# Sliding-window attention with ALiBi and an ELU MLP on one core: from two stages to one hand-ordered interleaving

## The chip, the core and the metric

The kernel runs on one of the eight cores of a Trainium2 chip. The core has five engines with an instruction queue each: TensorE (PE, matmuls; its weight loads are shown as PEld), VectorE (DVE), ScalarE (ACT), GpSimd (POOL) and SyncE (SP, which here only issues DMAs). They work on SBUF, the on-chip memory of 128 partitions, and on PSUM, eight banks of 128 x 512 f32 into which PE writes. The engines run side by side and wait for each other through semaphores; each runs its own instructions in their order. The metric is the time of one execution in microseconds of the device.

## What is computed

Attention over 8 batches, 8 heads, 576 positions, head size 64, in a causal window of 128 with a linear bias (ALiBi), then for all 4608 tokens an MLP 512 to 2048 to 512 with ELU (called MoE in the code, though it has one expert). Cut to what matters:

```python
scores = scale * np.matmul(q, k.transpose(0, 1, 3, 2))          # scale = 1 / sqrt(64) = 0.125
rel = pos[:, None] - pos[None, :]
slopes = 2.0 ** (-8.0 * (np.arange(H) + 1) / H)
bias = slopes[:, None, None] * (-np.abs(rel))[None, :, :]
mask = (rel >= 0) & (rel < 128)
attn = softmax(np.where(mask, scores + bias[None], -1e9))       # over keys
x = (attn @ v).transpose(0, 2, 1, 3).reshape(4608, 512)
h = x @ w_in
out = np.where(h > 0.0, h, np.exp(np.minimum(h, 0.0)) - 1.0) @ w_out
```

Inputs and output are f32 in device memory; the matmuls take f16.

## The kernel before

Scores are kept transposed, keys on partitions and queries along the free dimension. The 576 positions are four key blocks of 128 and one of 64. A key block sees queries of its own block and the next, so a head's scores are 128 rows of 256+256+256+192+64 = 1024 columns (`CUM` and `WID` are their starts and widths).

There are two stages, and the second begins when the first has ended. The Tile framework's scheduler sets the order of each engine's queue from the order in which the operations are written and the buffers of the pools; it also makes all semaphores.

Setup: POOL and DVE make an identity matrix and for each head a table `Mh` of bias and mask (L67), 128 x 256. POOL issues the loads of the weights, cast to f16 on the way (L76 for `w_in`, L81 for `w_out`).

Attention, for each batch: POOL issues the loads of q, k and v, cast to f16 (L130, L134, L141, L146). v goes into two tiles, each with 64 columns of ones beside the 64 of v (L140), so that the same matmul that makes the weighted values makes the softmax's denominators. For each pair of heads PE transposes q and k (L158) and ACT copies them to SBUF (L163 to L166). For each head: five score matmuls into PSUM `sp` (L174); DVE scales them and adds bias and mask, three operations `u` (L182, L186, L190); ACT takes Exp into `E` (L194, L195). One head later `do_av` follows: six matmuls of `E` with v and ones into `avp` (L108). For even heads DVE takes the reciprocal of the denominators (L114). For odd heads ACT takes Ln and then Exp of its negative (L117, L118), each with a load of another activation table ahead of it. DVE multiplies and writes the normalized values into `xT` (L119), which holds x transposed, 512 features by 4608 tokens, in f16.

MoE, for each of nine blocks of 512 tokens: for each of 16 chunks of 128 hidden features four matmuls make `hpsum` (L221, four PSUM buffers), ACT takes Relu (`rh`, L229) and Exp (`e`, L231), and DVE makes ELU from both as min(e - 1, rh) (`g`, L233): for h > 0 the smaller is h, for others it is e^h - 1, as the Relu is 0. Two chunks behind, four matmuls (L214) add the chunk into the four accumulators `opsum`, one for each 128 tokens. At a block's end ACT copies these to SBUF (`ob`, L241) and SP issues the stores.

## Time and profile before

| | |
|---|---|
| median of 3 runs | 573.47 us (573.37 to 573.53) |
| span of the profiled execution | 571.8 us, first to last instruction, so some 1.7 us lie around it |
| busy: PE, DVE, ACT, POOL | 448.8, 360.2, 405.4, 192.1 us |
| first matmul | at 26.0 us |
| first MoE matmul | at 308.8 us |
| last attention matmul | ends at about 311 us |
| moved by DMA | 46.14 MB read from device memory, 9.44 MB written |

How to read the profile: a group's row names line, engine, operation, output and inputs, their shapes and the count; behind it stand the time that the group was busy, the mean duration of one in ns, and how long its engine stood idle ahead of such instructions, with what ended that idle time. A line of the windows has the stretch and its length, then busy time and count for PE, PEld, DVE, ACT and POOL, then PE's granted clock, the busy share of the DMA engines and GB/s. A line of the timeline has start, duration from the first to the end of the last, engine, line, operation and count of a run of like instructions. Matmuls overlap: one starts while the one before it still drains, so their durations add up to more than the time that they take.

### The profile page before, as it was taken

Reading aid. Unit: us, or ns where it says so; the run is one execution under the profiler, and the core shown is the slowest. Engines: PE = TensorE matmul, PEld = TensorE weight load, DVE = VectorE, ACT = ScalarE, POOL = GpSimd, SP = SyncE. Lnnn points to the kernel's source line nnn. Section 1 sums busy time; section 2 is a strip of 40 time slices with the busy share of each in tenths; the row PEclk is TensorE's granted clock in tenths of the full one; section 3 lists DMA queues with packets and bytes.
Section 4 is the critical chain, followed back from the end, with each engine's and each line's share of the span. In section 5 each row is a group of like instructions: output and inputs, shape, how many; then the busy total and the mean of one; then the engine's idle time right before and its main releaser. Section 6 shows DMA issues by size and latency. Waiting matters only on the chain.

```text
span 571.8 us, 6352 instructions
## 1 busy us (share of the span) xinstructions
PE 448.8 (78%) x2176; PEld 211.4 (37%) x2176; DVE 360.2 (63%) x442; ACT 405.4 (71%) x709; POOL 192.1 (34%) x285
## 2 busy tenths in 40 slices
PE   0065667767767767767767999999999999999995
PEld 0033333333333333333433444444444444444442
DVE  2047899999999999999998534343434343433342
ACT  0036888888888888888888666666666767676764
POOL 5899996838659384780000000000000000000000
PEclk9999999999999999999999999999999999999999
DMA  7999999959999496990000001101010101010101
GB/s 150 188 109 116 94 106 69 93 33 101 66 71 82 29 107 44 84 83 0 0 1 1 1 37 39 52 23 64 11 74 1 73 1 74 1 73 1 75 1 74
DMA packets 158112, 32.92 MB, mean 58 GB/s; under 512 B 150912, under 2 KB 152960, under 8 KB 158080
## 3 DMA queue, kind: packets, MB, share of 16 engines
q0 software_dynamic: 152896, 23.08, 56.0%
q1 hardware_dynamic: 5184, 9.44, 4.4%
q8 instruction: 17, 0.28, 0.2%
q14 instruction: 15, 0.12, 0.1%
HBM read 46.14 MB, written 9.44 MB: 97 GB/s over the span
## 4 chain that ended last, share of the span: by engine, by line
PE 52%; DVE 29%; ACT 6%; issue 6%; POOL 3%; DMA 3%; ACTq 0%; POOLq 0%
PE opsum L214 21%; DVE rden L114 19%; PE hpsum L221 17%; PE avp L108 7%; PE tp L158 7%; DVE xT L119 4%; DVE u L182 2%; ACT ob L241 2%; DVE u L186 2%; DMA wi<-in_moe_w_in_dram 2%; DVE g L233 1%; ACT e L231 1%; PE sp L174 1%; POOL wo L81 1%; DMA ks<-in_k_dram 1%
## 5 line engine op out<-in xcount | busy, mean ns | idle before, releaser
L233 DVE SCALAR_TENSOR_TENSOR g<-e,rh 128x512 f16<-128x512 f32 x144 | 99.5, 692 | 149.1 <-ACT e L231 149.1
L214 PE MATMUL opsum<-wo,g 128*128 128x512 f16 x576 | 146.2, 379 | 2.4 <-DVE g L233 2.4
L221 PE MATMUL hpsum<-xT,wi 128*128 128x512 f16 x576 | 148.0, 383 | 0.0
L229 ACT ACTIVATE rh<-hpsum 128x512 f16<-128x512 f32 x144 | 87.5, 608 | 70.6 <-PE hpsum L221 69.6
L114 DVE RECIPROCAL rden<-avp 64x576 f32<-64x576 f32 x32 | 120.3, 3761 | 12.6 <-PE avp L108 11.3
L158 PE MATMUL tp<-ident,qs 128*128 128x128 f16 (+1 forms) x160 | 25.4, 291 | 89.8 <-DVE u L190 62.0
L108 PE MATMUL avp<-E,vts 128*128 128x256 f16 (+3 forms) x384 | 80.5, 335 | 14.3 <-ACT E L194 13.1
L231 ACT ACTIVATE e<-hpsum 128x512 f32<-128x512 f32 x144 | 87.2, 605 | 0.0
L214 PEld LDWEIGHTS <-g 128*128 128x128 f16 x576 | 54.9, 98 | 74.6 <-DVE g L233 11.5
L221 PEld LDWEIGHTS <-wi 128*128 128x128 f16 x576 | 56.7, 99 | 68.8 <-issue 1.9
L182 DVE SCALAR_TENSOR_TENSOR u<-sp,Mh 128x768 f32<-128x768 f32 x64 | 61.3, 957 | 31.1 <-PE sp L174 29.7
L194 ACT ACTIVATE E<-u 128x960 f16<-128x960 f32 x64 | 64.2, 1003 | 22.6 <-DVE u L186 22.5
L174 PE MATMUL sp<-qT,kT 64*128 64x256 f16 (+2 forms) x320 | 73.1, 368 | 8.0 <-ACT kT L165 5.2
L141 POOL DMA_DIRECT2D vts<-in_v_dram x64 | 57.7, 902 | 0.0
L108 PEld LDWEIGHTS <-vts 128*128 128x128 f16 (+1 forms) x384 | 36.4, 118 | 56.0 <-issue 42.6
L119 DVE TENSOR_TENSOR xT<-avp,rden 64x576 f16<-64x576 f32 x64 | 48.3, 754 | 8.8 <-ACT rden L118 5.6
L174 PEld LDWEIGHTS <-kT 64*128 64x128 f16 (+1 forms) x320 | 36.0, 126 | 42.9 <-issue 17.5
L158 PEld LDWEIGHTS <-qs 128*128 128x128 f16 (+1 forms) x160 | 14.5, 124 | 100.4 <-DVE u L190 47.0
L163 ACT COPY qT<-tp 128x512 f16<-128x512 f16 x32 | 18.4, 574 | 38.1 <-PE tp L158 38.1
L130 POOL DMA_DIRECT2D qs<-in_q_dram x32 | 28.1, 896 | 44.9 <-PE tp L158 44.7
L117 ACT ACT_TABLE_LOAD x32 | 41.1, 1283 | 0.6
L118 ACT ACT_TABLE_LOAD x31 | 39.8, 1283 | 0.6
(34 smaller groups left out, 311.8 us busy)
## 6 DMA issues: line engine op xcount, KB each, us to landing
out_dram<-ob SPq DMA_DIRECT2D x36, 256.0 KB, 2.4
vts<-in_v_dram POOLq DMA_DIRECT2D x64, 128.0 KB, 3.7
qs<-in_q_dram POOLq DMA_DIRECT2D x32, 128.0 KB, 4.3
ks<-in_k_dram POOLq DMA_DIRECT2D x32, 128.0 KB, 4.2
wi<-in_moe_w_in_dram POOLq DMA_DIRECT2D x4, 512.0 KB, 7.7
wo<-in_moe_w_out_dram POOLq DMA_DIRECT2D x16, 128.0 KB, 4.9
vts<-in_v_dram POOLq DMA_DIRECT2D x16, 64.0 KB, 3.1
qs<-in_q_dram POOLq DMA_DIRECT2D x8, 64.0 KB, 3.9
```

The lines of the kernel that those rows point to most:

```text
L108: nc.tensor.matmul(avp[:, a0:a1], vts[hh][0:nk, kb, hloc, :], em, start=st_, stop=sp_,)
L114: nc.vector.reciprocal(out=rden[o64:o64 + 64, :], in_=avp[o64:o64 + 64, 0:576])
L119: nc.vector.tensor_tensor(out=xT[hp_][p64:p64 + 64, b_ * S:(b_ + 1) * S], in0=avp[p64:p64 + 64, 0:576], in1=rden[o64:o64 + 64, :], op=ALU. ...
L158: nc.tensor.transpose(tp[:, which * NKB + kb, 0:nkk], src[0:nkk, kb, 2 * hp:2 * hp + 2, :], ident[0:nkk, 0:nkk],)
L174: nc.tensor.matmul(sp[0:nk, CUM[kb]:CUM[kb] + WID[kb]], kT2[p64:p64 + D, kb * 128: kb * 128 + nk], qT2[p64:p64 + D, kb * 128: kb * 128 + W ...
L182: nc.vector.scalar_tensor_tensor(out=u[:, 0:768], in0=sp[:, 0:768], scalar=0.125, in1=_bcast_mid(Mh[h % H], 3), op0=ALU.mult, op1=ALU.add,)
L194: nc.scalar.activation(E[:, 0:960], u[:, 0:960], AF.Exp)
L214: nc.tensor.matmul(opsum[ts], glist[fc][:, ts * 128:(ts + 1) * 128], w_out_sb[fc], start=(fc == 0), stop=(fc == 15),)
L221: nc.tensor.matmul(hp_, w_in_sb[kc][:, fc * 128:(fc + 1) * 128], xT[kc][:, tb * TB:(tb + 1) * TB], start=(kc == 0), stop=(kc == 3),)
L229: nc.scalar.activation(rh, hp_, AF.Relu)
L231: nc.scalar.activation(e, hp_, AF.Exp)
L233: nc.vector.scalar_tensor_tensor(out=g, in0=e, scalar=1.0, in1=rh, op0=ALU.subtract, op1=ALU.min)
```

## The change

The two stages become one row of 181 slots. All engines' queues are in the order written in the loop over slots (`manual_schedule`); Tile still makes the semaphores and buffers.

A pair of heads is a unit, and a unit begins every four slots (`APS`), so a batch takes 16 (`ABS`). Block t's hidden chunk fc stands in slot 21 + 16t + fc (`LAG` = 21), and its output matmuls 16 slots later, four in each slot. So slots 0 to 20 have attention alone, 21 to 36 attention and hidden chunks, 37 to 130 attention, hidden chunks and outputs, 131 to 164 hidden chunks and outputs, 165 to 180 outputs. Within a slot the order is: hidden chunk, ELU of the chunk before, attention's tasks, loads, output.

What else differs in the work:

- The bias enters through the contraction. `QK` holds each head's q and k in rows 0 to 63 and in rows 64 to 127 constant rows, made once: key position times slope against 1, 1 times slope against minus query position, and rows of indicators against -30000 that push keys ahead of their query far down. All score matmuls contract over 128 rows. ACT takes Exp straight from PSUM, scaled by 0.125. The exact window is cut afterwards by DVE: a minimum of `E` with `band`, which is 60000 inside the window and 0 outside (`cut`).
- q and k are loaded four positions to a run of 1 KB (f32), so blocks hold positions in a permuted order that the last operations of attention undo. `transposes` copies by DVE, where ACT did it before.
- v is loaded once, in f32, by SP, and cast by POOL into `VP`, which has the ones between an even and an odd head's values.
- Scores of a head are two PSUM tiles of one bank; `ps_s` has two banks in turn for scores and transposes. The last 64 queries of all heads of a batch are collected in one bank (`values_tail`).
- All denominators go through Ln and Exp on ACT, and one activation table that has both is loaded once. No reciprocal and no Relu is left.
- ELU: ACT takes Exp of the hidden chunk, POOL clamps it to [0, 1], DVE takes max(e - 1, h) with h from PSUM. `hp` has two PSUM buffers.
- An output accumulator is one bank: 16 matmuls over four slots for 128 tokens, a copy by ACT, a store by SP.

The diff, cut to its core (the old attention and MoE loops are removed whole):

```diff
-    with tc.tile_pool(name="astage", bufs=2) as astage, \
...
-    TB = 512
...
+    NP = H // 2
+    NFC = FF // 128
+    NTB = NTOK // 512
+    APS = 4
+    ABS = NP * APS
+    LAG = ABS + 5
+    MID = S // 2
...
+    work = ctx.enter_context(tc.tile_pool(name="work", bufs=3))
+    gpool = ctx.enter_context(tc.tile_pool(name="gpool", bufs=2))
+    ps_s = ctx.enter_context(tc.tile_pool(name="ps_s", bufs=2, space=PSUM))
+    ps_v = ctx.enter_context(tc.tile_pool(name="ps_v", bufs=2, space=PSUM))
+    ps_t = ctx.enter_context(tc.tile_pool(name="ps_t", bufs=1, space=PSUM))
+    ps_h = ctx.enter_context(tc.tile_pool(name="ps_h", bufs=2, space=PSUM))
+    ps_o = ctx.enter_context(tc.tile_pool(name="ps_o", bufs=1, space=PSUM))
...
+    QK = const.tile([128, H, 2, 768], F16, name="QK")
+    VP = [const.tile([128, 5, NP, 256], F16, name=f"VP{g}", tag=f"VP{g}") for g in range(2)]
+    w_in_sb = [const.tile([128, FF], F16, name=f"wi{c}", tag=f"wi{c}") for c in range(4)]
+    w_out_sb = const.tile([128, NFC, DM], F16, name="wo")
+    xT = const.tile([128, 4, NTOK], F16, name="xT")
...
+    def cast_v(b, n):
+        p = 128 if n < 4 else 64
+        nc.gpsimd.tensor_scalar(
+            out=VP[b % 2][0:p, n, :, :].rearrange("p a (g c) -> p (a g) c", g=2)[:, :, 0:64],
+            in0=vf.pop((b, n))[0:p, :, :], scalar1=1.0, scalar2=0.0, op0=ALU.mult, op1=ALU.add)
+    nc.scalar.preload_act_table_set("natural_log_exp_and_others")
+    with tc.manual_schedule():
+        for hp in range(NP):
+            for f in load_qk(0, (2 * hp, 2 * hp + 2)):
+                f()
+        for f in load_tail(0):
+            f()
+        make_identity(nc, ident)
...
+        nc.vector.memset(band, BIG)
+        def keep(cols, pattern, base, cm):
+            for h in range(4):
+                r = slice(32 * h, 32 * h + 32)
+                o = band[r, cols]
+                if len(pattern) > 1:
+                    o = o.rearrange("p (n j i) -> p n j i", j=4, i=32)
+                nc.gpsimd.affine_select(out=o, in_=o, compare_op=ALU.is_ge, fill=0.0,
+                                        base=base(h), pattern=pattern, channel_multiplier=cm)
...
+        for t, pr, one in ((TQ, 96, 64), (TK, 64, 96)):
+            nc.vector.memset(t[one:one + 1, :], 1.0)
+            nc.vector.tensor_scalar(
+                out=t[pr:pr + 1, :], in0=posi[pr:pr + 1, :],
+                scalar1=(-1.0 if pr == 96 else 1.0), scalar2=None, op0=ALU.mult)
+        nc.vector.memset(QK[:, :, 1, 512:768], 0.0)
+        for h in range(H):
+            c = 8.0 * 2.0 ** (-8.0 * (h + 1) / H)
+            for w, t, sc in ((1, TK, c), (0, TQ, 1.0)):
+                for d0, s0, n in ((0, 0, 576), (640, 512, 64)):
+                    if h % 2:
+                        nc.vector.tensor_scalar(
+                            out=QK[64:128, h, w, d0:d0 + n], in0=t[64:128, s0:s0 + n],
+                            scalar1=sc, scalar2=None, op0=ALU.mult)
+                    else:
+                        nc.scalar.mul(QK[64:128, h, w, d0:d0 + n], t[64:128, s0:s0 + n], sc)
+        for g in range(2):
+            nc.vector.memset(VP[g][:, 4, :, :], 0.0)
+            nc.vector.memset(VP[g][:, :, :, 64:128], 1.0)
+        for n in range(3):
+            load_v(0, n)
+        for n in range(5):
+            cast_v(0, n)
+            if n < 2:
+                load_v(0, n + 3)
...
+        def transposes(b, hp):
+            t = ps_s.tile([128, 2, 2, 4, 2, 32], F16, name="tp", tag="sps")
+            for g in range(2):
+                for w in (1, 0):
+                    for j in range(2):
+                        nc.tensor.transpose(
+                            t[:, g, w, :, j, :],
+                            stq[b][:, w, 2 * hp + g, 2 * j:2 * j + 2, :].rearrange("p a d -> p (a d)"),
+                            ident)
+            for odd in range(2):
+                r = slice(64 * odd, 64 * odd + 64)
+                nc.vector.tensor_copy(
+                    QK[0:64, 2 * hp:2 * hp + 2, :, 0:512].rearrange(
+                        "p h w (n a i) -> p (h w) n a i", a=2, i=32)[:, :, :, odd, :],
+                    t[r, :, :, :, :, :].rearrange("p h w n a i -> p (h w) (n a) i"))
...
+        def scores(b, hp, g, half):
+            s = ps_s.tile([128, 512], F32, name="sp", tag="sps")
+            kq = QK[:, 2 * hp + g, :, :]
+            c0 = 512 + 128 * (b % 2)
+            if half == 0:
+                mm = [(0, 0, 0, 256), (128, 256, 128, 256)]
+            else:
+                mm = [(256, 0, 256, 256), (384, 256, 384, 128), (384, 384, c0, 64), (c0, 448, c0, 64)]
+            for kc, o, qc, n in mm:
+                nc.tensor.matmul(s[:, o:o + n], kq[:, 1, kc:kc + 128], kq[:, 0, qc:qc + n],
+                                 start=True, stop=True)
+            if half == 0:
+                ex[b, hp, g] = work.tile([128, 1024], F16, name="E", tag="E")
+            nc.scalar.activation(ex[b, hp, g][:, 512 * half:512 * half + 512], s, AF.Exp, scale=0.125)
+        def cut(b, hp, g):
+            e = ex[b, hp, g]
+            nc.vector.tensor_tensor(out=e, in0=e, in1=band, op=ALU.min)
+        def values(b, hp, g):
+            e = ex[b, hp, g]
+            vp = VP[b % 2]
+            a = avt[b, hp, g] = ps_v.tile([128, 512], F32, name="av", tag="av")
+            lo = 64 * g
+            for n, o0, e0, w, st, sp in ((0, 0, 0, 256, True, False), (2, 256, 512, 256, False, False),
+                                         (1, 128, 256, 256, False, False), (3, 384, 768, 128, False, True)):
+                nc.tensor.matmul(a[:, o0:o0 + w], vp[:, n, hp, lo:lo + 128], e[:, e0:e0 + w],
+                                 start=st, stop=sp)
...
+        def log_den(b, hp, g):
+            if g == 0:
+                lden[b, hp] = work.tile([128, 512], F32, name="lden", tag="lden")
+            r = slice(64, 128) if g == 0 else slice(0, 64)
+            nc.scalar.activation(lden[b, hp][r, :], avt[b, hp, g][r, :], AF.Ln)
+        def inv_den(b, hp):
+            rden[b, hp] = work.tile([128, 512], F32, name="rden", tag="rden", bufs=2)
+            nc.scalar.activation(rden[b, hp], lden.pop((b, hp)), AF.Exp, scale=-1.0)
+        def normalize(b, hp, g):
+            r, o = (slice(0, 64), slice(64, 128)) if g == 0 else (slice(64, 128), slice(0, 64))
+            nc.vector.tensor_tensor(
+                out=xT[r, hp, b * S:b * S + 512].rearrange("p (n i j) -> p n j i", j=4, i=32),
+                in0=avt.pop((b, hp, g))[r, :].rearrange("p (n j i) -> p n j i", j=4, i=32),
+                in1=rden[b, hp][o, :].rearrange("p (n j i) -> p n j i", j=4, i=32), op=ALU.mult)
...
+        def hidden(t, fc):
+            p = hps[t, fc] = ps_h.tile([128, 512], F32, name="hp", tag="hp")
+            for c in range(4):
+                nc.tensor.matmul(p, w_in_sb[c][:, fc * 128:(fc + 1) * 128],
+                                 xT[:, c, t * 512:(t + 1) * 512], start=(c == 0), stop=(c == 3))
+            e = es[t, fc] = work.tile([128, 512], F32, name="e", tag="e")
+            nc.scalar.activation(e, p, AF.Exp)
+            nc.gpsimd.tensor_scalar(out=e, in0=e, scalar1=1.0, scalar2=0.0, op0=ALU.min, op1=ALU.max)
+        def elu(t, fc):
+            if t not in gs:
+                gs[t] = gpool.tile([128, NFC, 512], F16, name="g")
+            nc.vector.scalar_tensor_tensor(
+                out=gs[t][:, fc, :], in0=es.pop((t, fc)), scalar=1.0, in1=hps.pop((t, fc)),
+                op0=ALU.subtract, op1=ALU.max)
...
+        def output(t, i):
+            ts, f0 = i // 4, 4 * (i % 4)
+            if f0 == 0:
+                ops[t] = ps_o.tile([128, DM], F32, name="op", tag="op")
+            for fc in range(f0, f0 + 4):
+                nc.tensor.matmul(ops[t], gs[t][:, fc, ts * 128:(ts + 1) * 128], w_out_sb[:, fc, :],
+                                 start=(fc == 0), stop=(fc == NFC - 1))
+            if f0 == 12:
+                ob = work.tile([128, DM], F32, name="ob", tag="ob")
+                nc.scalar.copy(ob, ops[t])
+                r0 = t * 512 + ts * 128
+                nc.sync.dma_start(out[r0:r0 + 128, :], ob)
...
+        units = [(b, hp) for b in range(B) for hp in range(NP)]
+        for u, (b, hp) in enumerate(units):
+            s = APS * u
...
+            at(s, scores, b, hp, 0, 0)
+            at(s, scores, b, hp, 0, 1)
+            at(s + 1, cut, b, hp, 0)
+            if u + 1 < len(units):
+                at(s + 1, transposes, *units[u + 1])
+            if hp == 2 and b + 1 < B:
+                at(s + 3, transposes_tail, b + 1)
+            at(s + 2, scores, b, hp, 1, 0)
+            at(s + 3, values, b, hp, 0)
+            at(s + 3, log_den, b, hp, 0)
+            at(s + 3, scores, b, hp, 1, 1)
+            at(s + 4, cut, b, hp, 1)
+            at(s + 5, values, b, hp, 1)
+            at(s + 5, log_den, b, hp, 1)
+            at(s + 5, inv_den, b, hp)
+            at(s + 5, values_tail, b, hp)
+            at(s + 6, normalize, b, hp, 0)
+            at(s + 6, normalize, b, hp, 1)
+            if hp == NP - 1:
+                at(s + 6, normalize_tail_den, b)
+                at(s + 6, normalize_tail, b)
...
+        for b in range(1, B):
+            for n in range(5):
+                at(ABS * (b - 1) + 2 + 2 * n, load_v, b, n)
+                at(ABS * (b - 1) + 6 + 2 * n, cast_v, b, n)
...
+        transposes_tail(0)
+        transposes(0, 0)
+        nslots = LAG + NTB * NFC + NFC
+        for s in range(nslots):
+            m = s - LAG
+            if 0 <= m < NTB * NFC:
+                hidden(m // NFC, m % NFC)
+            if 0 <= m - 1 < NTB * NFC:
+                elu((m - 1) // NFC, (m - 1) % NFC)
+            for f in tasks.get(s, []):
+                f()
+            for l in loads.get(s, []):
+                do_load(*l)
+            if 0 <= m - NFC < NTB * NFC:
+                output((m - NFC) // NFC, (m - NFC) % NFC)
```

Two places show how the queues change. The first is VectorE. In the program before, at the end of attention, one head's bias (`u`), the reciprocal, the last two normalizations and all the ELU operations `g` behind them stand so:

```order
L182 SCALAR_TENSOR_TENSOR u<-sp,Mh_92 128x768
L186 SCALAR_TENSOR_TENSOR u<-sp,Mh_92 128x192
L190 SCALAR_TENSOR_TENSOR u<-sp,Mh_92 64x64
L114 RECIPROCAL rden<-avp 64x576
L119 TENSOR_TENSOR xT_137<-avp,rden 64x576 x2
L233 SCALAR_TENSOR_TENSOR g<-e,rh 128x512 x144
```

In the changed program VectorE has in the middle of the row, over one unit (`E` are the exponentials that are cut, `g` the ELU results, `tp` and `tpt` the transposes):

```order
L325 SCALAR_TENSOR_TENSOR g_2095<-e_2179,hp_2174 128x512
L288 TENSOR_TENSOR xT_92<-av_2123,rden_2189 64x4x4x32
L288 TENSOR_TENSOR xT_92<-av_2183,rden_2189 64x4x4x32
L325 SCALAR_TENSOR_TENSOR g_2095<-e_2217,hp_2212 128x512
L231 COPY QK_84<-tpt_2244 64x4x2x64 x2
L325 SCALAR_TENSOR_TENSOR g_2095<-e_2240,hp_2235 128x512
L253 TENSOR_TENSOR E_2226<-E_2226,band_83 128x1024
L325 SCALAR_TENSOR_TENSOR g_2095<-e_2280,hp_2275 128x512
L253 TENSOR_TENSOR E_2288<-E_2288,band_83 128x1024
L215 COPY QK_84<-tp_2327 64x4x8x32 x2
```

The ELU operations have moved from behind all of attention to one in each slot, between the cuts, copies and normalizations of a unit.

The second place is POOL near the start. Before, the loads of the weights stand there, with the two mask operations:

```order
masks.py:199 AFFINE_SELECT ident<-ident 128x128
L56 AFFINE_SELECT vmask<-vmask 128x256
L76 DMA wi_94<-in_moe_w_in_dram 128x2048
L60 AFFINE_SELECT vmask<-vmask 128x256
L76 DMA wi_96<-in_moe_w_in_dram 128x2048
```

In the changed program POOL has first issued the loads of batch 0's q and k, and made `band` (36 operations) and the constant rows `TK` and `TQ`; the end of that, the casts of batch 0's v, and the weights stand so:

```order
L173 AFFINE_SELECT TQ_152<-TQ_152 32x2x128
L173 AFFINE_SELECT TQ_152<-TQ_152 32x64
L105 TENSOR_SCALAR VP0_85<-vf_224 128x8x64
L105 TENSOR_SCALAR VP0_85<-vf_229 128x8x64
L105 TENSOR_SCALAR VP0_85<-vf_234 128x8x64
L105 TENSOR_SCALAR VP0_85<-vf_240 128x8x64
L105 TENSOR_SCALAR VP0_85<-vf_246 64x8x64
L381 DMA wi0_87<-in_moe_w_in_dram 128x2048
L381 DMA wi1_88<-in_moe_w_in_dram 128x2048
```

The weights' loads have moved behind q, k, the constant rows and the casts.

338 lines of the change are left out of this document (145 added, 193 removed).

## The prediction

> **What bounds the kernel now.** I read the page first (busy time per engine, the chain that ended last), then the windows by stage, then the groups by shape inside each stage, and last the timeline at a few places. The page:
>
> ```profile
> PE 448.8 (78%) x2176; PEld 211.4 (37%) x2176; DVE 360.2 (63%) x442; ACT 405.4 (71%) x709; POOL 192.1 (34%) x285
> PE 52%; DVE 29%; ACT 6%; issue 6%; POOL 3%; DMA 3%; ACTq 0%; POOLq 0%
> ```
>
> No engine is full over the whole span. The shares are averages over two stages with different limits, as the windows show (busy us of PE, PEld, DVE, ACT, POOL in each stretch):
>
> ```profile
> 0.00:34.00 34.00, 2.77 (x10) 1.03 (x10) 3.40 (x10) 2.23 (x4) 25.65 (x47) 1.00 1.36 166
> 34.00:302.00 268.00, 188.08 (x993) 96.63 (x994) 245.42 (x277) 221.57 (x371) 166.47 (x239) 1.00 1.03 66
> 302.00:314.00 12.00, 8.54 (x33) 3.47 (x32) 10.35 (x10) 9.75 (x13) 0.00 (x0) 1.00 0.00 1
> 314.00:320.00 6.00, 5.38 (x26) 2.32 (x25) 4.79 (x7) 4.95 (x10) 0.00 (x0) 1.00 0.00 0
> 320.00:563.00 243.00, 241.44 (x1109) 107.10 (x1108) 95.54 (x138) 163.87 (x309) 0.00 (x0) 1.00 0.10 35
> 563.00:572.00 9.00, 2.62 (x12) 0.81 (x10) 0.69 (x1) 3.03 (x6) 0.00 (x0) 0.88 0.31 117
> ```
>
> There are 34 us of loading, 280 us of attention (to 314) and 258 us of MoE. In attention DVE is busy 245.42 of 268 us and PE waits for it; in MoE PE is busy 241.44 of 243 and DVE is idle 60% of the time. The groups by shape, attention (40 to 300) first and MoE (316 to 562) second; columns are busy us, mean ns, idle before:
>
> ```profile
> L114 DVE RECIPROCAL rden<-avp 64x576 f32<-64x576 f32 x30 | 112.8, 3761 | 12.0 <-PE avp L108 10.8
> L108 PE MATMUL avp<-E,vts 128*128 128x256 f16 x180 | 60.0, 401 | 10.9 <-ACT E L194 9.7 <-DMA vts<-in_v_dram 1.2
> L182 DVE SCALAR_TENSOR_TENSOR u<-sp,Mh 128x768 f32<-128x768 f32 x60 | 57.5, 958 | 1.4
> L119 DVE TENSOR_TENSOR xT<-avp,rden 64x576 f16<-64x576 f32 x60 | 45.3, 754 | 6.8 <-ACT rden L118 3.6
> L117 ACT ACT_TABLE_LOAD x30 | 38.5, 1283 | 0.5
> L186 DVE SCALAR_TENSOR_TENSOR u<-sp,Mh 128x192 f32<-128x192 f32 x60 | 21.1, 352 | 0.4
> L117 ACT ACTIVATE lden<-avp 64x576 f32<-64x576 f32 x30 | 19.3, 643 | 16.4 <-PE avp L108 16.3
> L108 PE MATMUL avp<-E,vts 128*128 128x64 f16 x59 | 15.4, 261 | 0.0
> L221 PE MATMUL hpsum<-xT,wi 128*128 128x512 f16 x555 | 141.3, 379 | 0.0
> L233 DVE SCALAR_TENSOR_TENSOR g<-e,rh 128x512 f16<-128x512 f32 x142 | 98.1, 692 | 147.1 <-ACT e L231 147.0
> L231 ACT ACTIVATE e<-hpsum 128x512 f32<-128x512 f32 x141 | 85.4, 606 | 0.0
> L221 PEld LDWEIGHTS <-wi 128*128 128x128 f16 x554 | 54.2, 98 | 65.3
> L241 ACT COPY ob<-opsum 128x512 f32<-128x512 f32 x32 | 16.4, 600 | 9.7 <-PE opsum L214 9.7
> ```
>
> The reciprocal alone is 3.76 us per second head. The other thing to see is PE: 256 columns take 401 ns in attention, 512 columns 379 ns in MoE. The timeline gives the distance between starts (whole run less the last matmul, over the rest):
>
> ```profile
> 204.96 0.63 PE L108 MATMUL avp<-E,vts 128*128 128x256 f16 x2
> 204.96 1.29 PE L108 MATMUL avp<-E,vts 128*128 128x256 f16 x6
> 206.06 0.57 PE L158 MATMUL tp<-ident,ks 128*128 128x128 f16 x3
> 310.78 1.47 PE L221 MATMUL hpsum<-xT,wi 128*128 128x512 f16 x3
> 345.93 1.03 PE L221 MATMUL hpsum<-xT,wi 128*128 128x512 f16 x4
> 346.79 1.03 PE L214 MATMUL opsum<-wo,g 128*128 128x512 f16 x4
> 347.66 1.03 PE L221 MATMUL hpsum<-xT,wi 128*128 128x512 f16 x4
> L221 PE MATMUL hpsum<-xT,wi x576: 379/379/634, 308.8 to 562.5; 128*128 128x512 f16 x192
> ```
>
> At 345.93: (1.03-0.38)/3 = 0.217 us for 512 columns, 0.424 ns a column. At 204.96: 0.63-0.42 = 0.21 us for 256; at 310.78, with the longest duration 0.634 of the last row: (1.47-0.63)/2 = 0.42 for 512; both 0.83 ns a column. So PE runs all of attention at half the speed of MoE, though the clock column of the windows says 1.00 in both; and it speeds up at about 314, some 3 us after matmuls begin to run without a break at 310.78. A 64-column matmul is limited otherwise: the last of the six begins at 204.96+1.29-0.26 = 205.99 and the next starts at 206.06, 0.07 us.
>
> **The change part by part.** What goes: 32 reciprocals (120 us), 192 bias operations on DVE (64 x (0.958+0.352) = 84, and a short one each), the table loads (38.5 for half of them), 144 Relu passes on ACT. What comes on DVE: a minimum over 128x1024 per head and two copies of 64x1024 per pair out of PSUM. On POOL: 144 clamps of 128x512 and the casts of v. PE keeps its 1152 MoE matmuls and gets 34 per pair of heads (12 of 256 columns, 12 of 128, 10 of 64: 5248 columns). The program is a row of 181 slots; I cost it in six stretches.
>
> *D, slots 37 to 130 (94 slots), all work interleaved.* Four slots hold one pair (a unit). PE: eight 512-column matmuls a slot take 347.66-345.93 = 1.73 us; the unit's 34 cost 12 x 0.109 + 22 x 0.07 = 2.85, so (4 x 1.73 + 2.85)/4 = 2.44 a slot. The floor is all of them at 0.424 ns a column, 2.22 a unit; the ceiling adds a bare weight load to each, 34 x 0.098 = 3.3 on 2.2, 3.1 a slot with one short wait. DVE: a line through L182 and L186 is 0.15 us + 1.05 ns an element, so 1.23 us for 1024. Four g (2.77), two normalizations (1.38, as g), two minima and two copies (4.92), a quarter of the tails (0.55): 9.6, or 2.40 a slot. Minima and copies have f16 operands, which no DVE row shows; if they ran at double rate they would be 0.69 each and DVE 1.85. I take values between, since the nearest rows are all f32. ACT: eight passes of 0.606, two Ln of 0.6, one Exp and one copy of 0.6: 7.2, or 1.8. POOL, from the rows below: clamps 4 x 0.71, casts 0.9, DMA issues 0.8: 4.5, or 1.1. PE is the longest by little. It restarts after waits for cut scores, for copies and for g; before, such a restart is 0.18 (row at 564.76 below). One per slot: 2.62, **D = 246**, bounds 229 and 291. The hp buffers don't set it: only two, but hidden 1.03, e 0.61, clamp 0.71, g 0.69 and hand-overs of 0.4 are 3.44 us against two slots of 5.2; the slot with two copies ahead of the next g uses up most of that slack.
>
> The start and the end need these rows:
>
> ```profile
> 0.86 0.27 DVE L55 MEMSET vmask<- 128x256 f32 x1 [0.86 <-PEq L257]
> 0.97 0.34 POOL L51 IOTA deltai<- 128x256 int32 x1
> 1.27 0.29 POOL masks.py:199 TENSOR_SCALAR_AFFINE_SELECT ident<-ident 128x128 f16<-128x128 f16 x1
> 1.51 0.45 POOL L56 TENSOR_SCALAR_AFFINE_SELECT vmask<-vmask 128x256 f32<-128x256 f32 x1
> 4.54 2.15 POOL L81 DMA_DIRECT2D wo<-in_moe_w_out_dram  x4
> 20.82 3.52 POOL L130 DMA_DIRECT2D qs<-in_q_dram  x4 [0.17 <-issue]
> 24.31 0.73 POOL L134 DMA_DIRECT2D qs<-in_q_dram  x1
> 564.76 1.04 PE L214 MATMUL opsum<-wo,g 128*128 128x512 f16 x4 [0.18 <-DVE g L233]
> 565.19 2.05 ACT L241 COPY ob<-opsum 128x512 f32<-128x512 f32 x4 [1.21 <-PE opsum L214]
> out_dram<-ob SPq DMA_DIRECT2D x36, 256.0 KB, 2.4
> ```
>
> The two select rows (and their starts: 0.40 from the second to what follows) make POOL about 0.15 us + 1.1 ns an element, 0.71 for 512; a memory fill would be cheaper, and up to double is possible for a clamp of two steps.
>
> *A, to the first score.* q and k now come ahead of the weights, so loading no longer bounds. POOL's row does: ten issues (8 x 0.54 + 2 x 0.73 = 5.8), identity 0.5, 28 selects of 256 or 128 (24 x 0.45 + 4 x 0.29 = 12), eight of 64 (1.8), two iotas (0.8), 15 operations on TK and TQ (10 x 0.45 + 5 x 0.22 = 5.6): with the first 0.7, 27 us. DVE waits for the last, then in its order fills QK (16 pieces; 4 to 8 us), sets VP (2 to 4), its small steps (2 to 4), and copies the first transposes (2.5 to 3.8): 10 to 19, so **A = 42**, 37 to 46. The weights queue behind the casts on POOL; the last of these waits for VP on DVE, so they start near 40 and have until slot 21 (76 us) to land: with batch 1's q and k 5.4 MB in f16, and before, the first 34 us moved 166 GB/s x 34 = 5.6 MB.
>
> *B, slots 0 to 20, attention alone.* PE is at half speed (0.83 ns). Between one minimum and the next of its kind: values 0.75, tails 0.3, transposes 8 x 0.107, two copies 1.4 to 2.5, scores 0.43, Exp 0.61, minimum 0.69 to 1.23, hand-overs 0.6: 5.6 to 7.2 a unit. 5.25 units x 6.4: **B = 34**, 29 to 38. *C, slots 21 to 36, no output matmuls yet:* DVE 1.85 to 2.40 a slot, or PE at half speed (16 x 0.42 + 4.4)/4 = 2.8; I take 2.4: **C = 38**, 30 to 45. *E, slots 131 to 164, MoE alone:* PE 1.73, the two hp buffers 3.44/2 = 1.72, I take 1.78: **E = 60.5**, 59 to 72. The bufs were four before; this cover is gone, and each 0.1 us more in the clamp costs 34 x 0.05 = 1.7. *F, the last 16 slots:* 16 x 0.865 + three turns of the single op bank (drain 0.2, copy 0.6, 0.1) 2.7 + last copy 0.6 + landing 2.4 + close 2.2 (571.8 less 565.19+2.05+2.4): **F = 22**.
>
> Sum: 42+34+38+246+60.5+22 = 442.5 of span. The span before is 571.8 and the median of runs 573.47, 1.7 around it: 444.
>
> A rule against the change stands in the Trainium skill, "GPSIMD Engine Reference", sections 1 and 8: POOL shares its SBUF interfaces with DVE and they contend when a DVE instruction has two SBUF inputs, which the minimum has and g no longer has. No trace here shows both at once. By it, as an estimate, a clamp could be late by a whole minimum; the sum would stay where the slack above covers it.
>
> **The rivals.** (1) POOL's clamp is slow, 1.5 us or more, by its own rate or by the minima holding it up. For: no row has a two-step operation of POOL. Against: the selects. E becomes (2.73+1.5)/2 = 2.1 a slot, +11; in D the late g holds DVE's row and through it a few tenths a slot, 0.2 x 94 = 19: 475. Chance 0.12. (2) The slots don't overlap: each PE wait for DVE or ACT stands in the slot, which is then 1.73 + 6.4/4 = 3.33; D = 313 and the time 511. For: PE's order is fixed, one late operand stops all behind it. Against: every consumer stands at least a slot behind its producer. Chance 0.07. (3) The copies and minima at double rate, short matmuls by columns alone: A 37, B 30, C 30, D 94 x 2.35 = 221, E 59, F 22, 401. Chance 0.06. (4) Slower: PE stays at half speed because short waits break its runs, as in attention before. Then D = 94 x (8 x 0.42 + 1.1) = 419, E = 34 x 3.36 = 114, F 35, C 45, A and B 76: 691. It decides from the point where (573-444)/(691-444) = 0.52 of the work runs so. For: attention before, busy for 188 of 268 us and still half. Against: at half speed D needs 4.46 a slot of PE, far above any other engine, so PE would run unbroken, and that is what raised it at 314. Chance 0.04. The Trainium skill, "TensorE: Matmul & The Clock Gate", Part 1, says that the array's clock is halved by default, released after about 3.4 us of sustained work, and halved again after an idle window; the trace agrees on the release (some 3 us), and shows no second halving in the MoE stage. By this rule rival 4 can only strike stretches with long idle times, A and B, where it stands in the sum already, and C, which would be 45 instead of 38.
>
> **How the numbers follow.** The forecast has 0.70; its terms span 411 to 517 if all fall together, 425 to 470 by independent misses. Range 415 to 492: it takes in rival 1 and leaves out 2, 3 and 4, 0.17. A measurement of this kernel tells about 0.2% from no change. Faster 0.95 (forecast, 1, 2, 3), same 0.01 (rival 4 for about half the time), slower 0.04.
>
> **What would show it.** PE busy nearly all of D with 512-column matmuls of 379 ns, DVE about 85%; first score near 42, first hidden near 76, last attention near 360, output-only from 421. A mean near 630 ns for hidden means rival 4; g waiting for POOL in D means rival 1; PE waiting for DVE in each slot, rival 2. It is wrong if D's slot is outside 2.4 to 3.0 us.

## The result and the profile after

The changed kernel took 432.6 us (median of 4 runs, 431.75 to 432.81) against 573.44 for the kernel before beside it: a ratio of 0.754, with a 95% interval of 0.753 to 0.7552. The forecast was 444. The profiled execution took 432.81 with a span of 431.1, so 1.7 us lie around it, as before.

From the page of the kernel after, the engines, the clock that was granted to TensorE in 40 slices of 10.8 us, and the chain that ended last:

```profile
PE 343.0 (80%) x2240; PEld 187.6 (44%) x2240; DVE 287.7 (67%) x396; ACT 241.8 (56%) x445; POOL 169.8 (39%) x289
PEclk9999955699999999999999999999999999999999
PE 49%; DVE 30%; POOL 8%; DMA 5%; issue 4%; ACT 3%; POOLq 0%; ACTq 0%; DVEq 0%
```

PE is busy for 106 us less, though it does more matmuls: the attention matmuls now run at the full clock but for a stretch early on. The windows of the kernel after, cut at the forecast's stages A to F (the first score, the first hidden chunk, slots 37, 131 and 165, the end):

```profile
0.00:43.70 43.70, 1.57 (x16) 1.23 (x17) 13.03 (x32) 7.11 (x17) 36.97 (x82) 1.00 0.49 78
43.70:79.30 35.60, 21.03 (x166) 15.63 (x167) 25.25 (x32) 20.61 (x37) 9.82 (x14) 0.69 1.28 194
79.30:118.30 39.00, 27.75 (x203) 16.28 (x202) 32.84 (x44) 24.73 (x47) 15.99 (x24) 0.93 0.57 78
118.30:349.30 231.00, 219.10 (x1527) 121.72 (x1525) 189.97 (x251) 160.43 (x297) 85.60 (x136) 1.00 0.36 70
349.30:409.10 59.80, 58.27 (x270) 26.27 (x269) 25.60 (x38) 25.41 (x45) 20.81 (x34) 1.00 0.10 36
409.10:431.10 22.00, 15.27 (x68) 6.44 (x66) 0.96 (x2) 3.52 (x6) 0.61 (x1) 0.96 0.16 60
```

The second column is each stage's length. Beside the forecast:

| stage | forecast | after | difference |
|---|---|---|---|
| A, to the first score | 42 | 43.7 | +1.7 |
| B, slots 0 to 20 | 34 | 35.6 | +1.6 |
| C, slots 21 to 36 | 38 | 39.0 | +1.0 |
| D, slots 37 to 130 | 246 (2.62 a slot) | 231.0 (2.457) | -15.0 |
| E, slots 131 to 164 | 60.5 | 59.8 | -0.7 |
| F, the end | 22 | 22.0 | 0 |

The miss is D's; against its -15.0, A to C have 4.3 more. PE is busy for 219.1 of its 231.0 us (95%), DVE for 190.0 (82%). The groups by shape of the kernel after (busy us, mean ns, idle before) show the durations that the forecast had to bound:

```profile
L316 PE MATMUL hp<-xT,wi 128*128 128x512 f16 x576 | 149.5, 382 | 23.7 <-DVE g L325 23.6
L325 DVE SCALAR_TENSOR_TENSOR g<-e,hp 128x512 f16<-128x512 f32 x144 | 97.1, 687 | 67.9 <-POOL e L320 66.0
L320 POOL TENSOR_SCALAR e<-e 128x512 f32<-128x512 f32 x144 | 90.0, 625 | 216.8 <-ACT e L319 209.1 <-DMA vf<-in_v_dram 6.9
L288 DVE TENSOR_TENSOR xT<-av,rden 64x512 f16<-64x512 f32 x64 | 83.5, 1304 | 2.0
L253 DVE TENSOR_TENSOR E<-E,band 128x1024 f16<-128x1024 f16 x64 | 44.0, 688 | 7.6 <-ACT E L249 7.6
L215 DVE COPY QK<-tp 64x1024 f16<-64x1024 f16 x64 | 44.0, 688 | 15.0 <-PE tp L209 14.4
L231 DVE COPY QK<-tpt 64x512 f16<-64x512 f16 x16 | 6.6, 415 | 0.1
```

Minimum (L253) and copy (L215) take 0.69 us for 1024 elements, little more than half of the 1.23 worked out from f32 rows. The normalization (L288), taken as 0.69 like `g`, takes 1.30 and is DVE's second largest group. The clamp (L320) takes 0.63 where 0.71 was taken. Hidden matmuls take 382 ns on average: 379 in D, and over 600 only for the first eight, before 85 us, which run at half clock.

### The profile page after: what moved, and what is told of

Same layout as the page of the kernel before. It is cut to its first block, busy times and chain, and to the rows that moved or that the text cites. A ratio compares the mean times of both kernels' runs of the same rounds, so it can differ in the third digit from the quotient of the medians.

```text
span 431.1 us, 6246 instructions
## 1 busy us (share of the span) xinstructions
PE 343.0 (80%) x2240; PEld 187.6 (44%) x2240; DVE 287.7 (67%) x396; ACT 241.8 (56%) x445; POOL 169.8 (39%) x289
## 4 chain that ended last, share of the span: by engine, by line
PE 49%; DVE 30%; POOL 8%; DMA 5%; issue 4%; ACT 3%; POOLq 0%; ACTq 0%; DVEq 0%
PE hp L316 20%; PE op L337 18%; DVE xT L288 13%; DVE g L325 7%; DVE QK L215 7%; DMA stt<-in_q_dram 4%; PE av L262 4%; POOL band L128 3%; PE sp L245 3%; PE tp L209 2%; POOL stq L76 2%; DVE xT L306 1%; DVE E L253 1%; DMA vf<-in_v_dram 1%; ACT e L319 1%
## 5 line engine op out<-in xcount | busy, mean ns | idle before, releaser
L320 POOL TENSOR_SCALAR e<-e 128x512 f32<-128x512 f32 x144 | 90.0, 625 | 216.8 <-ACT e L319 209.1
L316 PE MATMUL hp<-xT,wi 128*128 128x512 f16 x576 | 149.5, 382 | 23.7 <-DVE g L325 23.6
L319 ACT ACTIVATE e<-hp 128x512 f32<-128x512 f32 x144 | 86.0, 597 | 111.6 <-PE hp L316 109.0
L337 PE MATMUL op<-wo,g 128*128 128x512 f16 x576 | 145.9, 379 | 2.9 <-ACT ob L341 2.9
L325 DVE SCALAR_TENSOR_TENSOR g<-e,hp 128x512 f16<-128x512 f32 x144 | 97.1, 687 | 67.9 <-POOL e L320 66.0
L288 DVE TENSOR_TENSOR xT<-av,rden 64x512 f16<-64x512 f32 x64 | 83.5, 1304 | 2.0
L249 ACT ACTIVATE E<-sp 128x512 f16<-128x512 f32 x128 | 72.5, 595 | 7.1 <-PE sp L245 6.3
L245 PE MATMUL sp<-QK 128*128 128x256 f16 (+2 forms) x384 | 47.4, 249 | 30.6 <-issue 27.4
L215 DVE COPY QK<-tp 64x1024 f16<-64x1024 f16 x64 | 44.0, 688 | 15.0 <-PE tp L209 14.4
L253 DVE TENSOR_TENSOR E<-E,band 128x1024 f16<-128x1024 f16 x64 | 44.0, 688 | 7.6 <-ACT E L249 7.6
```

The source lines that it names most:

```text
L215: nc.vector.tensor_copy(QK[0:64, 2 * hp:2 * hp + 2, :, 0:512].rearrange("p h w (n a i) -> p (h w) n a i", a=2, i=32)[:, :, :, odd, :], t[r ...
L245: nc.tensor.matmul(s[:, o:o + n], kq[:, 1, kc:kc + 128], kq[:, 0, qc:qc + n], start=True, stop=True)
L249: nc.scalar.activation(ex[b, hp, g][:, 512 * half:512 * half + 512], s, AF.Exp, scale=0.125)
L253: nc.vector.tensor_tensor(out=e, in0=e, in1=band, op=ALU.min)
L288: nc.vector.tensor_tensor(out=xT[r, hp, b * S:b * S + 512].rearrange("p (n i j) -> p n j i", j=4, i=32), in0=avt.pop((b, hp, g))[r, :].rea ...
L316: nc.tensor.matmul(p, w_in_sb[c][:, fc * 128:(fc + 1) * 128], xT[:, c, t * 512:(t + 1) * 512], start=(c == 0), stop=(c == 3))
```

## The experiments

The times below stand beside the kernel before on the same chip, with the 95% interval of the ratio. Some expectations put D's slot in the kernel after at 2.49 us; by the windows above it is 2.457.

**Attention ahead of the MLP (e3_attention_first).** One line puts the first hidden chunk behind the last unit, so that everything is recoded as in the kernel after and nothing is interleaved.

```diff
-    LAG = ABS + 5
+    LAG = B * ABS + 5
```

> The changed kernel with the MoE row shifted behind all of attention (LAG 133 instead of 21), so nothing is interleaved, the operations being the same. Theory: the interleaving carries most of the gain. 43.7 to the first score, then 33 units at the 7 us that a unit takes alone (PE at half speed, waiting for DVE) = 233, the 144 hidden slots at 1.73 = 249, the end 22: about 548, so of the 141 us gained about 25 are left. Rival: the lighter attention carries it (no reciprocal, no bias on DVE, no table loads); then attention alone runs at 5 us a unit and the time is below 490.

Measured 558.67 us, ratio 0.9743 [0.9723, 0.9762], nearer to the theory. The windows of this kernel, attention and MLP:

```profile
43.70:287.00 243.30, 146.62 (x1072) 108.68 (x1073) 179.52 (x216) 137.26 (x243) 46.56 (x64) 0.57 0.56 82
287.00:531.00 244.00, 233.25 (x1069) 104.22 (x1067) 99.66 (x144) 104.78 (x177) 85.88 (x140) 0.99 0.09 33
```

Attention alone takes 243.3 us for 32 units, 7.6 a unit, at a granted clock of 0.57, and no engine is full: DVE, the busiest, is busy for 74% of it. The unit is a chain from engine to engine. So of the 141 us that the change gains, the cheaper operations alone give 573.4 - 558.7 = 15, and putting the MLP's matmuls into the chain's waits gives 558.7 - 432.6 = 126. This is the share in that order, the operations first: no run interleaves the old operations, of which DVE's kept it busy for 245 of 268 us of attention.

**The kernel before without its reciprocal (e4_before_no_reciprocal).** All heads take the denominators through Ln and Exp on ACT, with one activation table for both loaded once.

```diff
+    nc.scalar.preload_act_table_set("natural_log_exp_and_others")
...
-            if hh == 0:
-                nc.vector.reciprocal(out=rden[o64:o64 + 64, :], in_=avp[o64:o64 + 64, 0:576])
-            else:
-                lden = aSm.tile([128, 576], F32, name="lden")
...
+            lden = aSm.tile([128, 576], F32, name="lden")
```

> The kernel before with one part of the change alone: all denominators through Ln and Exp on ACT, one activation table loaded once, no reciprocal. Theory: attention before is bounded by DVE through the reciprocal; a pair falls from 8.5 us to the 6.5 to 7.5 that ACT and PE at half speed need: 573 - 32 x 1.5 = 525, between 510 and 540. Rival: ACT takes over as the bound, since it gets 1.3 us more per pair and stood at 221 of 268; time above 550.

Measured 547.21 us, ratio 0.9543 [0.9524, 0.9562], between the theory and its rival. The waits of this kernel:

```profile
DVE xT L117 <- ACT rden L116: 109.2, 33, 3.7
```

The removed 120 us of DVE became a wait of 109.2 us for ACT's reciprocal: 26 of the 120 came out of the time. ACT did not get more to do, as the rival has it: a Ln and an Exp more for each pair (0.64 and 0.68 us), but two table loads of 1.28 less. No engine is full here either: ACT, the busiest, works for 190 of 241 us of attention (34 to 275). As in e3, a chain bounds attention that stands alone, and one long operation taken out shows the next link.

**A quarter of the first MLP matmul left out (e5_three_quarters).** This asks what sets D's slot. The hidden chunk contracts over three of its four feature chunks, so a quarter of that product is left out; PE's work falls by one 512-column matmul a slot, 0.217 us, and nothing else changes.

```diff
-            for c in range(4):
+            for c in range(3):
```

> The changed kernel with hidden chunks that contract over 384 of the 512 features (a quarter of the first MLP matmul is left out), so PE has 0.217 us less in each slot that has one. Theory: PE sets the pace of the interleaved stretch and of MoE alone, so D's slot falls from 2.49 to 2.28 or a little above and E's from 1.73 to 1.52 or to the 1.6 that the two hp buffers allow: 94 x 0.2 + 34 x 0.15 = 24 less, 409. Rival: DVE and the waits for g set D, PE only fills; D stays above 2.44 and the time above 422.

Measured 419.49 us, ratio 0.7317 [0.7302, 0.7331], nearer to the rival. The windows of this kernel for D and E, and its waits of PE in D:

```profile
119.90:341.50 221.60, 202.44 (x1431) 112.28 (x1430) 189.70 (x251) 158.42 (x296) 86.47 (x135) 1.00 0.38 73
341.50:396.00 54.50, 52.12 (x236) 22.93 (x235) 25.58 (x38) 25.45 (x44) 20.81 (x34) 1.00 0.11 39
```

```profile
PE hp L316 <- DVE g L325: 14.3, 23, 1.3
PE av L262 <- DVE xT L288: 4.9, 17, 0.3
```

D's slot falls from 2.457 to 221.6/94 = 2.357, 0.10 of the 0.217. PE is busy for 91% of D now, and the rest is wait for DVE: so D was not bounded by PE alone. What of DVE holds PE up is the question of the next three.

**The normalizations apart (e6_norm_spread).** The unit's second normalization comes one slot later. No duration changes.

```diff
-            at(s + 6, normalize, b, hp, 1)
+            at(s + 7, normalize, b, hp, 1)
```

> The changed kernel with the second normalization of a unit one slot later, so two of 1.30 us no longer stand ahead of the same g. Theory: what D's slot of 2.49 has above PE's 2.28 comes from g standing behind both; spread, the hidden matmuls wait less and the slot falls to 2.40 or below: 8 to 12 us less, 421 to 425. Rival: the wait moves to the next g and to the values matmuls, which need the bank that the later normalization holds; no more than 2 us either way, 431 to 435.

Measured 415.74 us, ratio 0.7258 [0.7245, 0.7272]: 17 us under the kernel after, more than expected; D gives 13 of them and C, 35.4 us long here, most of the rest. The timeline of the kernel after shows what it removes (start, duration, what the run waited for):

```profile
242.15 2.65 DVE L288 TENSOR_TENSOR xT<-av,rden 64x512 f16<-64x512 f32 x2
242.61 1.03 PE L316 MATMUL hp<-xT,wi 128*128 128x512 f16 x4
244.10 1.03 PE L337 MATMUL op<-wo,g 128*128 128x512 f16 x4
244.82 1.28 DVE L325 SCALAR_TENSOR_TENSOR g<-e,hp 128x512 f16<-128x512 f32 x2
245.56 1.02 PE L316 MATMUL hp<-xT,wi 128*128 128x512 f16 x4 [0.43 <-DVE g L325]
```

Two normalizations hold DVE for 2.65 us, longer than a slot. The `g` behind them comes late, and the hidden chunk two slots on needs that `g` to give back one of the two `hp` banks. The waits of PE for it in D, of the kernel after and then of this kernel:

```profile
PE hp L316 <- DVE g L325: 11.7, 17, 1.3
```

```profile
PE hp L316 <- DVE g L325: 0.6, 1, 0.6
```

They are nearly gone, and D is 217.7 us with PE busy for 217.06:

```profile
114.80:332.50 217.70, 217.06 (x1522) 121.32 (x1522) 193.80 (x252) 159.94 (x296) 86.70 (x135) 1.00 0.38 74
```

So DVE at 89% busy does not hold PE up when its long operations don't stand in a row.

**The normalization written in order (e1_norm_in_order).** It wrote `xT` four elements (8 bytes) apart. Here it writes in order, and takes both inputs 32 f32 (128 bytes) apart.

```diff
-                out=xT[r, hp, b * S:b * S + 512].rearrange("p (n i j) -> p n j i", j=4, i=32),
-                in0=avt.pop((b, hp, g))[r, :].rearrange("p (n j i) -> p n j i", j=4, i=32),
-                in1=rden[b, hp][o, :].rearrange("p (n j i) -> p n j i", j=4, i=32), op=ALU.mult)
+                out=xT[r, hp, b * S:b * S + 512].rearrange("p (n i j) -> p n i j", j=4, i=32),
+                in0=avt.pop((b, hp, g))[r, :].rearrange("p (n j i) -> p n i j", j=4, i=32),
+                in1=rden[b, hp][o, :].rearrange("p (n j i) -> p n i j", j=4, i=32), op=ALU.mult)
```

> The changed kernel with the normalization walking its output in order (the read from PSUM and of the reciprocals takes the strides instead). Theory: the 1.30 us of a normalization, forecast at 0.69, is the price of writing f16 eight bytes apart; in order it takes 0.69, g no longer waits behind two long ones, the hidden matmuls no longer wait for g, and the slot of the interleaved stretch falls from 2.49 to about 2.37 us: 94 slots give 11, the two stretches before some 6, 415 in all. Rival one: PE's row alone sets the interleaved stretch; normalizations get short, but only the stretches before gain: 426. Rival two: strided reading costs the same as strided writing; 1.30 stays, 432.

Measured 419.26 us, ratio 0.7309 [0.7298, 0.7319], between the theory and rival one; the group of this kernel:

```profile
L288 DVE TENSOR_TENSOR xT<-av,rden 64x512 f16<-64x512 f32 x64 | 66.7, 1042 | 2.0
```

The order of the write costs, as this is 0.26 us shorter although both reads now take strides; and 1.04 is not yet 0.69. Whether one of the two reads costs the rest is the next run's question.

**The reciprocal in order too (e9_rden_in_order).** With e1's write and its read of PSUM, ACT writes `rden` in the output's order, so that only the operand in PSUM is read 128 bytes apart.

```diff
-            nc.scalar.activation(rden[b, hp], lden.pop((b, hp)), AF.Exp, scale=-1.0)
+            nc.scalar.activation(
+                rden[b, hp].rearrange("p (n i j) -> p n i j", j=4, i=32),
+                lden.pop((b, hp)).rearrange("p (n j i) -> p n i j", j=4, i=32), AF.Exp, scale=-1.0)
...
+                in1=rden[b, hp][o, :].rearrange("p (n i j) -> p n i j", j=4, i=32), op=ALU.mult)
```

> The kernel with normalizations that write in order, and besides with the reciprocals put in that order by ACT's Exp, so of a normalization's operands only the one in PSUM is read with strides. Theory: the 1.05 us that was left is the strided read of the SBUF operand; it falls to 0.69 and the time by 3 to 8 more, 411 to 416. Rival: it is the strided read from PSUM; 1.05 stays and 419 with it. A third case: ACT's Exp gets longer by its own strides.

Measured 410.73 us, ratio 0.7167 [0.7155, 0.7179], just under the theory's 411 to 416. The groups of this kernel, the windows of its D:

```profile
L290 DVE TENSOR_TENSOR xT<-av,rden 64x512 f16<-64x512 f32 x64 | 44.1, 689 | 2.4 <-ACT rden L284 0.5
L284 ACT ACTIVATE rden<-lden 128x512 f32<-128x512 f32 x32 | 35.5, 1110 | 1.0
```

```profile
111.30:327.70 216.40, 215.80 (x1526) 121.92 (x1524) 163.22 (x251) 171.98 (x297) 84.88 (x135) 1.00 0.38 75
```

The normalization is at the forecast's 0.69. The reordering moved to ACT, whose Exp now takes 1.11 us, and there it hides: PE is busy for 215.8 of D's 216.4 us. That is PE's floor, 216.4/94 = 2.302 us a slot.

**The band behind TK and TQ (e2_band_later).** POOL makes `band` after the tables that the first score needs, not ahead of them: the block from `memset(band)` to its last `keep` moves behind the loop that makes `TK` and `TQ`.

> The changed kernel with POOL making the constant rows TK and TQ ahead of the window band instead of behind it. Theory: POOL's row sets the start, so DVE gets TK and TQ 15.8 us earlier and the first score comes at 28 to 31 instead of 43.7; the casts of v still end near 38 and take some of it back: 420 to 424. Rival: the loads or the casts set the start; the first values wait as long as the scores gain, and the time stays above 429.

Measured 435.85 us, ratio 0.7597 [0.7579, 0.7615]: 3 us slower than the kernel after, as the rival had it. The windows of A and B, and the waits between the first score and the first hidden chunk, of this kernel:

```profile
0.00:29.20 29.20, 1.61 (x17) 1.29 (x18) 14.31 (x32) 7.12 (x17) 25.95 (x60) 1.00 0.49 68
29.20:81.40 52.20, 24.43 (x166) 17.10 (x167) 25.50 (x32) 20.76 (x37) 20.98 (x36) 0.73 1.06 164
```

```profile
PE tpt L224 <- DMA stt<-in_q_dram: 12.8, 1, 12.8
PE av L262 <- POOL VP L105: 4.8, 3, 2.6
DVE E L253 <- POOL band L163: 3.0, 1, 3.0
```

The first score comes 14.5 us sooner, and B takes 16.6 longer. POOL's queue also holds the casts of v and, behind these, the issue of the second batch's loads; PE waits for the last of those for 12.8 us, with the wanted work queued behind.

**The start in another order (e7_start).** The same, with what e2 ran into taken out of the way: the first batch's v is cast by DVE, ahead of the fill of `QK`, with the memsets of `VP`; the second batch's q and k are issued ahead of the MLP weights.

```diff
+            cast_v(0, n, nc.vector)
...
-        for f in pre:
-            f()
         for f in load_qk(1) + load_tail(1):
             f()
+        for f in pre:
+            f()
```

> The kernel with the band behind TK and TQ, and besides with batch 0's v cast by DVE in its idle time at the start, VP set there too, and batch 1's q and k loaded ahead of the first MLP weights. Theory: the earlier first score (about 26) was lost to the wait for batch 1's tail loads (12.8 us) and to the casts; with both gone first hidden comes near 68 instead of 79: 420 to 423. Rival: something else in the first 80 us, the weights' landing at slot 21 say, is as late as before: above 429.

Measured 419.99 us, ratio 0.7325 [0.7304, 0.7345]: 13 us under the kernel after. The windows of A came to 27.8 us, and of B to:

```profile
27.80:66.20 38.40, 22.66 (x167) 16.87 (x168) 25.50 (x32) 20.78 (x37) 19.13 (x36) 0.94 1.01 161
```

A lost 15.9 us and B gained 2.8, as the first minimum now waits 4.9 us for `band`, which POOL makes later; from the first hidden chunk on, C is 0.6 shorter and the rest the same. So 13 of the 16 us of A stay gained when the casts leave POOL and the second batch's loads go ahead of the weights. Which of the two counts for how much was not run apart.

**Together (e10_together).** e9, e6 and e7 in one kernel.

> Three edits together: the reciprocal written by ScalarE in natural order and the normalization with a natural-order f16 write; the unit's second normalization one slot later; the start of the start-up experiment (TK and TQ ahead of the band, the first batch's v cast by VectorE, the second batch's q and k ahead of the MLP weights). Theory (the stage of slots 37 to 130 is bounded by TensorE at 2.28 us a slot once VectorE has room, and the start by the chain to the first score): first score at 28, first hidden at 64, slots 2.29 to 2.33 us, output-only stage and end as in the kernel after; 28 + 36 + 34 + 217 + 57 + 22 + 2 = 396 us, 391 to 400. Rival (what the two normalization edits gain is the same wait, and the start's gain is lost to the first batch's tail loads or to the clock): no better than 404, that is 6 us under the best single edit.

Measured 395.15 us, ratio 0.689 [0.6878, 0.6902], as the theory had it and the best of all. The windows of this kernel for B and D:

```profile
27.60:64.10 36.50, 24.45 (x166) 17.50 (x167) 20.85 (x32) 22.34 (x37) 19.14 (x36) 1.00 1.01 160
97.00:313.50 216.50, 215.90 (x1525) 121.94 (x1523) 163.85 (x252) 171.81 (x297) 85.71 (x136) 1.00 0.38 74
```

D is the same 216.5 as in e9: the two edits of the normalization remove the same wait, and PE's own work is left. The clock of 1.00 in B's row is not what PE ran at there; see below.

## Why the prediction was right, and where it was off

**What the change is worth.** The forecast had the direction, the size, and the reason: stages with two different limits laid over each other, with PE busy nearly throughout. By e3 this is 126 of the 141 us, and the removed reciprocals and bias operations alone are 15. How much the interleaving owes to these lighter operations is not shown.

**D, two terms off.** The slot was worked out as 2.44 of PE's work and 0.18 for one restart. PE's work was mis-sized: it measured 2.302 (e9, e10). The eight MLP matmuls were right at 1.73; the unit's 34 short ones were taken as 2.85 us from 64-column matmuls that start 0.07 apart at half clock, and measured (2.302 - 1.73) x 4 = 2.3. The timeline of the kernel after:

```profile
239.24 0.19 PE L273 MATMUL avtail<-E,VP 128*128 128x64 f16 x1
239.27 0.19 PE L274 MATMUL avtail<-E,VP 128*128 128x64 f16 x1
239.30 0.19 PE L273 MATMUL avtail<-E,VP 128*128 128x64 f16 x1
```

They start 0.03 us apart, what 64 columns take at 0.424 ns each (0.027). The nearest row was a row of the half clock, and the floor of 2.22 that the text named for columns alone was the better value. The 0.14 a slot is 13 of the 15 us.

The restart's size was nearly right, 2.457 - 2.302 = 0.155, but its cause wasn't the one named. The text had one per slot, after waits for cut scores, copies and `g`. In the runs it is `g` nearly alone, 17 times in 94 slots and up to 1.3 us long, 11.7 us in all, behind two normalizations in a row (e6). The step that failed is "two normalizations (1.38, as g)": they take 2.61. With the true 0.69 (e9) the wait is gone. And the sentence that the `hp` buffers don't set D was wrong: D's waits are for an `hp` bank. It had seen the thin slack, but put the two copies there, where the two normalizations stand.

DVE's sum came out between its two ends by two errors against each other: minima and copies ran at double rate (0.69, the end that the text did not take), which takes 2.2 us off a unit, and the normalizations add 1.2. 190.0/94 = 2.02 a slot, 82% busy, where the text said about 85%. (The text says that it takes values between; its 9.6 has the f32 price for all four. And its terms together span 408 to 516 by its own bounds, not 411 to 517. Neither moves the forecast.)

**A, right by two misses.** POOL was to be ready at 27 and ended at 31.3; the steps behind it were put at 10 to 19 and took 12.4. The timeline of the kernel after:

```profile
30.65 0.65 POOL L173 TENSOR_SCALAR_AFFINE_SELECT TQ<-TQ 32x256 f16<-32x256 f16 x2
43.72 1.01 PE L245 MATMUL sp<-QK 128*128 128x256 f16 x6 [27.40 <-issue]
```

**B and C** came near, 35.6 and 39.0 against 34 and 38, but by luck. The cycle that the text adds up for B has no normalization in it. The timeline of the kernel after has one, as the values matmuls wait for the `av` bank that it gives back:

```profile
65.14 0.69 DVE L253 TENSOR_TENSOR E<-E,band 128x1024 f16<-128x1024 f16 x1 [0.58 <-ACT E L249]
68.04 2.62 DVE L288 TENSOR_TENSOR xT<-av,rden 64x512 f16<-64x512 f32 x2
69.38 0.90 PE L262 MATMUL av<-E,VP 128*128 128x256 f16 x4 [2.37 <-DVE xT L288]
72.83 0.69 DVE L253 TENSOR_TENSOR E<-E,band 128x1024 f16<-128x1024 f16 x1 [0.58 <-ACT E L249]
```

From one minimum to the next of its kind this is 7.7 us, above the text's 5.6 to 7.2; in e10, with normalizations of 0.69, it is 7.1. B is not longer because the first such interval has no normalization (4.1 us) and the second, with one, ran mostly at full clock (6.7, from 49.52 to 56.19); the third waits 3.0 us for the second batch's loads and takes 9.0. In C the hidden matmuls wait 10.3 us for `g`, which the sum doesn't have; in e9 C takes 32.8 us.

So the half clock was a right ingredient of B, worth about 1 us of 7.7 by these two intervals. The windows don't show it well, as the text had found for the kernel before: their clock for B is 0.69 in the kernel after and 1.00 in e10. The score matmuls of 256 columns in B of the kernel after, in its D, and in B of e10:

```profile
L245 PE MATMUL sp<-QK 128*128 128x256 f16 x33 | 9.4, 359 | 30.6 <-issue 27.4 <-ACT E L249 3.1
L245 PE MATMUL sp<-QK 128*128 128x256 f16 x136 | 26.1, 273 | 0.0
L245 PE MATMUL sp<-QK 128*128 128x256 f16 x33 | 11.0, 407 | 11.7 <-ACT QK L199 9.8 <-ACT E L249 1.5 <-DVE QK L231 0.3
```

At 407 ns, as in attention before (401), all of e10's B ran at half speed; at 359, B of the kernel after was the faster of the two. What B would take at full clock, no run shows.

**E and F** came out within 1 us. In E, behind one wait of 1.5 us for `g` at its start, hidden chunks start 1.73 us apart, which is PE's own work; the two `hp` buffers, put at 1.72, do not set it. That is seen in e5, where a chunk has one matmul less and PE's work a slot is 1.73 - 0.217 = 1.51. The timeline of e5:

```profile
360.82 0.81 PE L316 MATMUL hp<-xT,wi 128*128 128x512 f16 x3
362.33 0.81 PE L316 MATMUL hp<-xT,wi 128*128 128x512 f16 x3
```

Chunks start 1.51 apart there, and every fourth time 1.70 to 1.74, when the output accumulator is copied out; `g` holds them up once, for 2.0 us, where attention ends. So a turn of two buffers takes no more than 3.02 us with three matmuls, and the text's 3.44 was too long.

**The rivals.** (1), the clamp: it takes 0.63. The contention that the text weighed can be seen and is small. Only 10 of the 144 clamps ran beside a minimum, and these were up to 0.94 long, 0.33 over the median, as here, in the timeline of the kernel after:

```profile
91.60 0.69 DVE L253 TENSOR_TENSOR E<-E,band 128x1024 f16<-128x1024 f16 x1
91.82 0.94 POOL L320 TENSOR_SCALAR e<-e 128x512 f32<-128x512 f32 x1 [0.28 <-ACT e L319]
```

and all of them together take 90.0 us, about 2 over 144 x 0.612, the median. In D the late `g` did hold PE up, as the rival's mechanism says, but DVE made it late and not POOL. (2), slots that don't overlap: e3's unit of 7.6 us in the place of 6.4 shows how long the chain is, and D's 2.457 that it lies beside PE's work. (3): both its premises held, double rate and short matmuls by columns alone, and its time of 401 did not, since A, B, C and the normalization were longer than it took. e9 has its D (216.4 against 221). (4), half clock throughout: not in D and E, where matmuls of 512 columns take 379 ns at a clock of 1.00. By the Trainium skill, "TensorE: Matmul & The Clock Gate", Part 1, the array is at half clock by default and after an idle window, and at full clock after sustained work. The trace of the kernel after agrees: matmuls run at half speed up to 85 us (most of B and the start of C), where attention starves PE, and at full speed behind it; e3 extends it, with half clock through most of 243 us in which PE is busy for 60%.

## What to carry to other kernels

When two stages have different limits and a chain of short operations bounds one of them, lay one over the other, and don't expect much of cheaper operations alone: here these were 15 of 141 us, and laying one over the other, once they were cheaper, was 126. After that, look for the longest run of operations in one engine's order that stands ahead of the one which gives a buffer back; placing them apart was worth 17 us without making anything faster. Price each operation by its access pattern and not by its element count, and price short matmuls at the clock that they will run at. Tell that clock by the durations of matmuls of one shape, not by the clock column alone.

## What the runs showed of the hardware

- DVE's multiply of 64x512 f32 from PSUM and SBUF into f16: 1.304 us when it writes 8 bytes apart and reads in order, 1.042 when it writes in order and reads both 128 bytes apart, 0.689 when only the PSUM operand is so read. In order throughout, the kernel before took 0.754 for 576 columns, so 0.69 for 512 at its 1.05 ns an element. So the PSUM read costs nothing here, the SBUF read 0.35 and the write 0.6. ACT's Exp of 128x512 goes from 0.63 to 1.11 with such a read from SBUF. The Trainium skill, "SBUF — State Buffer", section "SBUF: two separate sides", lets 16-bit elements lie up to 8 apart in SBUF for free and f32 up to 4: the f32 read here, 32 apart, agrees, and DVE's f16 write, 4 apart, does not.
- DVE's f16 minimum from SBUF and its f16 copy out of PSUM both take 0.688 us for 1024 elements, and the copy 0.415 for 512: 0.53 ns an element and 0.14 us, half of the 1.05 ns an element of the f32 rows of the kernel before.
- The granted clock in a profile's windows reads 1.00 where the trace has no clock record yet. The first record of the kernel after is at 47.2 us and of e10 at 67.7, so the 1.00 of A and of e10's B says nothing: there, 256-column matmuls took 407 ns, as at half clock. For the same reason the 0.69, 0.94 and 1.00 of B (after, e7, e10) can't be compared.
